# Modulation rows of the first LayerNorm loaded in blocks of 256, 512 and 256 columns, with the first chunk's start re-ordered, in an adaLN transformer block

## The chip, the cores and the metric

One Trainium2 chip, one of its NeuronCores. The metric is the device time in microseconds of one execution. The engines are named as in the profile: PE is TensorE (matrix multiplication), DVE is VectorE, ACT is ScalarE, POOL is GpSimd, SP is SyncE, which in this kernel only issues DMAs.

## What is computed

The reference is one transformer block with adaptive LayerNorm. Its core, cut to what matters:

```python
x = A_x                                             # 1 x 2048 x 1024, bf16
mod = (silu(c) @ w_mod).reshape(1, 6, 1, 1024)      # c: 1 x 1024, w_mod: 1024 x 6144
sa, ca, ga, sb, cb, gb = mod[:, 0] ... mod[:, 5]
h = layernorm(x) * (1 + ca) + sa
q, k, v = split(h @ wqkv)                           # 32 heads of 32
phi = lambda t: where(t > 0, t + 1, exp(t)) + 1e-6
kv = sum over s of phi(k) v;  z = sum over s of phi(k)
o = (phi(q) kv) / (phi(q) z + 1e-6)                 # linear attention
x = x + ga * (o @ wo)
h = layernorm(x) * (1 + cb) + sb
x = x + gb * ((silu(h @ w_gate) * (h @ w_up)) @ w_down)    # hidden width 3584
```

So before the first key can be computed, the kernel needs the LayerNorm statistics of the rows, the two vectors `sa` and `ca` (a matrix-vector product with the first 2048 columns of `w_mod`) and the key part of `wqkv`.

## The kernel before, in words

The 2048 rows of `x` are cut into four chunks of 512 (`NSC`), each of four row tiles of 128 (`STC`); the 1024 features are eight groups of 128 (`DC`), and every matrix product accumulates over these eight in one PSUM bank of 128 x 512. There are eight such banks. The order of all work is written out by hand: the kernel turns automatic scheduling off (line 130), each engine runs its instructions in the order in which the code states them, and only the waits between engines are put in by the framework. From line 423 on, a list `seq` gives the order of the big groups (values, queries, keys of the next chunk, feed-forward) and `put` hangs smaller steps behind them; the change does not touch that part.

What it touches is the head, lines 132 to 420, the first chunk up to its keys.

Loads. SP issues all of them on one queue (lines 133 to 161): `c`, then four row tiles of `x` (256 KB each), then, in turn, a pair of blocks of `w_mod` and two of the eight 128-row pieces of the key weights. `load_wme(p)` loads 256 columns for `ca` and 256 for `sa`, 512 KB each, in runs of 512 bytes; `load_wk(c0, c1)` loads pieces of 256 KB in runs of 2 KB. The first half of the value weights (`load_cols`, runs of 1 KB), row tiles 4 to 7, the other value half and the query weights follow (lines 375 to 381).

Row tiles. For each of the four, DVE takes statistics (`ln_stats`, L196 to L200), POOL makes the inverse deviation and the shift (L202, L204), and the tile is normalised (`ln_xn`): tiles 0, 1 and 3 on ACT (L214), tile 2 on POOL (L211). PE transposes each tile into a PSUM bank (`tr0`, L326; tile st uses bank st), and ACT or DVE copies it to `M4`, which holds the features on the partitions (`tr0_evac`, L332, L334).

Modulation. `mod_mm(p)` (L343) multiplies 256 columns of `ca` and 256 of `sa` with `silu(c)`: 32 matmuls with one moving column each, into a corner of bank 7. `mod_rows(p)` (L349 to L351) copies them out on DVE and adds 1 to `ca`; `modulate` (L224) applies scale and shift to a feature group of `M4` in place.

Keys. `kmm` (L242) is one 128 x 512 matmul of a key group (a row tile and one half of the key columns), for one feature group `cc`. There are eight key groups, 64 such matmuls. Groups 0 to 6 accumulate at once in banks 0 to 6, feature group by feature group, as the weights arrive; between them stand the four `mod_mm` and the transposes of tiles 2 and 3. Group 7 needs bank 7, which the modulation uses, so all its eight matmuls come last (lines 418 to 420). `k_evac` applies phi: ACT exponential (L237), DVE minimum and add (L238), DVE maximum and add (L239). The values (`v_group`, L257) follow at once, eight groups of eight matmuls that go through banks 0 to 4 in turn.

`warm(n)` (L187) issues n matmuls on zeros into bank 7; 21 stand at the start and 3 after the first transpose.

Of the kernel before, what the change touches and what calls it, by code (L numbers as in the profile page):

```python
# [10 lines left out]
BF16 = mybir.dt.bfloat16  # L11
# [10 lines left out]
def kernel(  # L22
# [13 lines left out]
    nc = tc.nc  # L36
    P = nc.NUM_PARTITIONS
    _, S, D = A_x.shape
# [3 lines left out]
    DC = D // P  # L42
# [24 lines left out]
    wm_v = w_mod.rearrange("(p j) n -> p j n", j=DC)  # L67
    c_v = c.rearrange("o (p j) -> p (o j)", j=DC)
# [8 lines left out]
    bank = [psum.tile([P, NB], F32, name=f"bank{i}") for i in range(8)]  # L77
# [9 lines left out]
    def view(region, off, shape, dtype=BF16):  # L87
        n = 1
        for s_ in shape:
            n *= s_  # L90
        w = n * (2 if dtype == F32 else 1)
        ap = region[:, off:off + w]
        if dtype == F32:
            ap = ap.bitcast(F32)
        if len(shape) == 2:
            ap = ap.rearrange("p (a b) -> p a b", a=shape[0])
        elif len(shape) == 3:
            ap = ap.rearrange("p (a b c) -> p a b c", a=shape[0], b=shape[1])
        return ap
# [6 lines left out]
    wme = view(M3, 0, [DC, 2 * D])  # L106
# [24 lines left out]


    c_sb = const.tile([P, DC], BF16, name="c_sb")
    nc.sync.dma_start(out=c_sb[:], in_=c_v)

    def load_x(st):
        nc.sync.dma_start(out=xs[st % 6], in_=x2[st * P:(st + 1) * P, :])

    def load_wme(p):
        for base in (D, 0):  # L140
            s_ = slice(base + p * 256, base + (p + 1) * 256)
            nc.sync.dma_start(out=wme[:, :, s_], in_=wm_v[:, :, s_])  # L142

    def load_wk(c0, c1):
        nc.sync.dma_start(out=wk[:, c0:c1, :], in_=wqkv_v[:, c0:c1, D:2 * D])  # L145

    def load_cols(dst, base, h):
        nc.sync.dma_start(out=dst[:, :, h * NB:(h + 1) * NB],
                          in_=wqkv_v[:, :, base + h * NB:base + (h + 1) * NB])

    for st in range(STC):
        load_x(st)
    load_wme(0)
    load_wk(0, 2)
    load_wme(1)
    load_wk(2, 4)
    load_wme(2)
    load_wk(4, 6)
    load_wme(3)
    load_wk(6, 7)  # L160
    load_wk(7, 8)

# [9 lines left out]
    saT = const.tile([P, DC], BF16, name="saT")  # L172
    ca1T = const.tile([P, DC], BF16, name="ca1T")
    sbT = const.tile([P, DC], BF16, name="sbT")
    cb1T = const.tile([P, DC], BF16, name="cb1T")
    m1 = const.tile([P, 6, DC], BF16, name="m1")
# [5 lines left out]
    scT = const.tile([P, DC], BF16, name="scT")  # L182
# [9 lines left out]
    def ln_stats(st):  # L192
        x_sb = xs[st % 6]
        stats = small.tile([P, NH, nc.vector.BN_STATS_DIM], F32, name="stats")
        for i in range(NH):
            nc.vector.bn_stats(out=stats[:, i, :], in_=x_sb[:, i * NB:(i + 1) * NB])  # L196
        mv = small.tile([P, nc.vector.BN_AGGR_DIM], F32, name="mv")
        nc.vector.bn_aggr(out=mv[:], in_=stats[:])
        veps = small.tile([P, 1], F32, name="veps")
        nc.vector.tensor_scalar_add(out=veps[:], in0=mv[:, 1:2], scalar1=LN_EPS)  # L200
        rstd = small.tile([P, 1], F32, name="rstd")
        nc.gpsimd.tensor_tensor(out=rstd[:], in0=veps[:], in1=neg_half[:], op=ALU.pow)  # L202
        nmr = small.tile([P, 1], F32, name="nmr")
        nc.gpsimd.tensor_scalar(out=nmr[:], in0=mv[:, 0:1], scalar1=rstd[:], scalar2=-1.0,  # L204
                                op0=ALU.mult, op1=ALU.mult)
        stat[st] = (rstd, nmr)

    def ln_xn(st, pool):
        rstd, nmr = stat.pop(st)
        if pool:  # L210
            nc.gpsimd.tensor_scalar(out=xns[st % 6], in0=xs[st % 6], scalar1=rstd[:], scalar2=nmr[:],  # L211
                                    op0=ALU.mult, op1=ALU.add)
        else:
            nc.scalar.activation(out=xns[st % 6], in_=xs[st % 6], func=ACT.Identity, scale=rstd[:], bias=nmr[:])  # L214
# [7 lines left out]
    def modulate(sc_, cc, sT, c1T, c0=0, c1=SCW):  # L222
        h = M4[:, sc_, cc, c0:c1]
        nc.vector.tensor_scalar(out=h, in0=h, scalar1=c1T[:, cc:cc + 1], scalar2=sT[:, cc:cc + 1],  # L224
                                op0=ALU.mult, op1=ALU.add)
# [9 lines left out]
    def phi_to(dst, acc):  # L235
        e = epool.tile([P, NB], F32, name="e")
        nc.scalar.activation(out=e[:], in_=acc, func=ACT.Exp)  # L237
        nc.vector.tensor_scalar(out=e[:], in0=e[:], scalar1=1.0, scalar2=PHI_EPS, op0=ALU.min, op1=ALU.add)  # L238
        nc.vector.scalar_tensor_tensor(out=dst, in0=acc, scalar=0.0, in1=e[:], op0=ALU.max, op1=ALU.add)  # L239

    def kmm(acc, sc_, t, h, cc):
        nc.tensor.matmul(acc[:], lhsT=M4[:, sc_, cc, t * P:(t + 1) * P], rhs=wk[:, cc, h * NB:(h + 1) * NB],  # L242
                         start=(cc == 0), stop=(cc == DC - 1))

    def k_evac(acc, t, h):
        phi_to(pk[:, t, h * NB:(h + 1) * NB], acc[:])
# [74 lines left out]


    def tr0(st):
        tp = bank[st][:].bitcast(BF16).rearrange("p (c s) -> p c s", c=DC)
        for cc in range(DC):
            nc.tensor.transpose(tp[:, cc, :], xns[st][:, cc * P:(cc + 1) * P], ident[:])  # L326

    def tr0_evac(st):
        tp = bank[st][:].bitcast(BF16).rearrange("p (c s) -> p c s", c=DC)
        dst = M4[:, 0, :, st * P:(st + 1) * P]  # L330
        if st % 2 == 0:
            nc.scalar.copy(out=dst, in_=tp)  # L332
        else:
            nc.vector.tensor_copy(out=dst, in_=tp)  # L334

    def mod_mm(p):
        mps = bank[7][:, p * 4:p * 4 + 4]
        for kind, base in enumerate((D, 0)):
            for i in range(2):
                col = base + (2 * p + i) * P  # L340
                o = kind * 2 + i
                for j in range(DC):
                    nc.tensor.matmul(mps[:, o:o + 1], lhsT=wme[:, j, col:col + P], rhs=scT[:, j:j + 1],  # L343
                                     start=(j == 0), stop=(j == DC - 1))

    def mod_rows(p):
        mps = bank[7][:, p * 4:p * 4 + 4]
        c2 = slice(2 * p, 2 * p + 2)
        nc.vector.tensor_copy(out=m1[:, 1, c2], in_=mps[:, 0:2])  # L349
        nc.vector.tensor_copy(out=saT[:, c2], in_=mps[:, 2:4])  # L350
        nc.vector.tensor_scalar_add(out=ca1T[:, c2], in0=m1[:, 1, c2], scalar1=1.0)  # L351

    warm(21)
    for st in range(STC):
        ln_stats(st)
    ln_xn(2, True)
    mask = const.tile([P, KVW], BF16, name="mask")
    nc.gpsimd.memset(mask[:], 0.0)
    for j in range(HPC):
# [3 lines left out]
    nc.gpsimd.memset(v_c[:, :, :, P:VW], 1.0)  # L363
    ln_xn(0, False)
    tr0(0)
    warm(3)
    ln_xn(1, False)
    tr0(1)
    tr0_evac(0)
    tr0_evac(1)  # L370
    mod_mm(0)
    mod_rows(0)
    modulate(0, 0, saT, ca1T, 0, 2 * P)
    modulate(0, 1, saT, ca1T, 0, 2 * P)
    tr0(2)
    ln_xn(3, False)
    load_cols(wv, 2 * D, 0)
    for st in range(STC, STC + 4):
# [1 line left out]
    load_cols(wv, 2 * D, 1)  # L380
    load_cols(wq, 0, 0)
    load_cols(wq, 0, 1)

    tr0_evac(2)
    G = [(t, h) for t in range(STC) for h in range(NH)]
    for g in (0, 1):
        for cc in (0, 1):
            kmm(bank[g], 0, G[g][0], G[g][1], cc)
    tr0(3)
    tr0_evac(3)  # L390
    modulate(0, 0, saT, ca1T, 2 * P, 4 * P)
    modulate(0, 1, saT, ca1T, 2 * P, 4 * P)
    for g in (2, 3):
        for cc in (0, 1):
            kmm(bank[g], 0, G[g][0], G[g][1], cc)
    mod_mm(1)
    mod_rows(1)
    for g in (4, 5, 6):
        for cc in (0, 1):
            kmm(bank[g], 0, G[g][0], G[g][1], cc)  # L400
    modulate(0, 2, saT, ca1T)
    modulate(0, 3, saT, ca1T)
    for p in (1, 2):
        k = 0
        for cc in (2 * p, 2 * p + 1):
            for g in range(7):
                kmm(bank[g], 0, G[g][0], G[g][1], cc)
                k += 1
                if k == 10:
                    mod_mm(p + 1)  # L410
                    mod_rows(p + 1)
                    modulate(0, 2 * p + 2, saT, ca1T)
                    modulate(0, 2 * p + 3, saT, ca1T)
    for g in range(7):
        for cc in (6, 7):
            kmm(bank[g], 0, G[g][0], G[g][1], cc)
        k_evac(bank[g], *G[g])
    for cc in range(DC):
        kmm(bank[7], 0, G[7][0], G[7][1], cc)
    k_evac(bank[7], *G[7])  # L420


    seq = []
# [264 lines left out]
```

## Time and profile before

| | |
|---|---|
| Median of 6 runs (lowest to highest) | 848.66 us (848.07 to 849.27) |
| The profiled execution's own time | 848.69 us |
| Span of its profile | 846.9 us, so 1.8 us lie around the span |
| PE busy | 834.3 us, 99% of the span, 4368 recorded instructions |
| DVE, ACT, POOL busy | 323.1, 143.9, 79.9 us |
| First value matmul (L257) starts | 32.65 us after the start of the span |
| 64 value matmuls | 32.65 to 46.46 us |

The profile's page gives busy time by engine, then the span in 40 slices of 21 us each, with the clock granted to PE and the share of the DMA engines; then the chain of work that ended last, and groups of instructions by source line. The trace behind it answers questions on a stretch of time: the instructions of one engine in order of time, with the idle time ahead of them and what ended it; the busy time of each engine in each of several short windows; and for DMAs the time from issue to landing. A recorded matmul of 128 x 512 lasts 379 ns because matmuls are pipelined; from start to start they take about 216 ns. Some matmuls are missing from the records.

### The profile page before, as it was taken

What the parts mean: (1) busy time and instruction counts of PE and PEld (TensorE: products, weight loads), DVE (VectorE), ACT (ScalarE), POOL (GpSimd) and SP (SyncE); (2) the same over time, 40 slices, a digit from 0 to 9 for tenths busy, and PEclk for the clock granted to TensorE, in tenths of its full rate; (3) what the DMA queues carried; (4) which work ended last, traced back from release to release, by engine and by line L of the source; (5) the groups of instructions that cost most, each with busy time, mean ns of one, the idle gap of its engine ahead of it and who ended that gap; (6) DMA issues with size and microseconds to landing.
All of it is one profiled execution on the core that took longest, in us unless ns stands there. A gap on an engine that the chain in (4) does not pass through costs nothing.

```text
span 846.9 us, 10893 instructions
## 1 busy us (share of the span) xinstructions
PE 834.3 (99%) x4368; PEld 396.6 (47%) x4452; DVE 323.1 (38%) x617; ACT 143.9 (17%) x269; POOL 79.9 (9%) x143
## 2 busy tenths in 40 slices
PE   8999999999999999999999999999999999999998
PEld 4454555544444444444444444444444444444444
DVE  5757455497755655422111221221122122112222
ACT  3333233322311111111111001111000111100000
POOL 2124030014122323100000000000000000000000
PEclk9999999999999999999999999999999999999999
DMA  9984982055489998877875215555322555201220
GB/s 279 317 243 116 283 191 64 1 118 159 98 212 218 217 220 212 193 244 240 246 236 179 69 52 171 149 151 149 106 75 69 151 154 157 86 15 66 75 69 26
DMA packets 203763, 128.65 MB, mean 152 GB/s; under 512 B 50496, under 2 KB 189888, under 8 KB 203712
## 3 DMA queue, kind: packets, MB, share of 16 engines
q1 hardware_dynamic: 163008, 98.58, 40.9%
q10 hardware_dynamic: 38400, 20.98, 11.7%
q0 software_dynamic: 2304, 8.39, 2.6%
q8 instruction: 35, 0.57, 0.3%
q14 instruction: 16, 0.13, 0.1%
HBM read 103.81 MB, written 12.58 MB: 137 GB/s over the span
## 4 chain that ended last, share of the span: by engine, by line
PE 95%; SPq 2%; DVE 1%; DMA 1%; issue 1%; ACT 0%; DVEq 0%
PE bank L515 23%; PE bank L534 23%; PE bank L509 23%; PE bank L466 7%; PE bank L265 6%; PE bank L257 6%; PE bank L242 5%; DMA M<-in_w_mod_dram 1%; SPq L145 1%; PE bank L439 1%; SPq L142 1%; PE bank L274 1%; PE bank L301 1%; DVE stats L196 0%; DVE M L239 0%
## 5 line engine op out<-in xcount | busy, mean ns | idle before, releaser
L515 PE MATMUL bank<-M,M 128*128 128x512 bf16 x881 | 210.4, 379 | 0.8
L509 PE MATMUL bank<-M,M 128*128 128x512 bf16 x871 | 209.7, 379 | 1.3
L517 DVE TENSOR_TENSOR M<-bank,e 128x512 bf16<-128x512 f32 x112 | 77.5, 692 | 275.1 <-PE bank L515 265.7
L534 PE MATMUL bank<-M,M 128*128 128x512 bf16 (+1 forms) x687 | 146.9, 370 | 0.6
L512 ACT ACTIVATE e<-bank 128x512 f32<-128x512 f32 x112 | 66.8, 597 | 439.7 <-PE bank L509 415.7
L534 PEld LDWEIGHTS <-M 128*128 128x128 bf16 x924 | 90.4, 98 | 103.3
L515 PEld LDWEIGHTS <-M 128*128 128x128 bf16 x896 | 87.7, 98 | 105.7
L509 PEld LDWEIGHTS <-M 128*128 128x128 bf16 x896 | 87.3, 98 | 103.9
L538 DVE TENSOR_TENSOR M<-bank,gb_bc 128x512 f32<-128x512 f32 (+1 forms) x33 | 22.3, 676 | 149.2 <-PE bank L534 135.3
L242 PE MATMUL bank<-M,M 128*128 128x512 bf16 x244 | 58.3, 382 | 1.1 <-DVE M L334 0.3
L466 PE MATMUL bank<-M,M 128*128 128x512 bf16 x254 | 57.8, 379 | 0.1
L265 PE MATMUL bank<-M,M 128*128 128x512 bf16 x250 | 56.7, 379 | 0.3
L257 PE MATMUL bank<-M,M 128*128 128x512 bf16 x250 | 56.2, 379 | 0.3
L237 ACT ACTIVATE e<-bank 128x512 f32<-128x512 f32 x64 | 37.8, 598 | 100.2 <-PE bank L265 48.4
L534 PE MATMUL bank<-M 128*128 128x512 bf16 x219 | 50.7, 379 | 0.3
L239 DVE SCALAR_TENSOR_TENSOR M<-bank,e 128x512 bf16<-128x512 f32 x64 | 44.3, 692 | 3.7
L238 DVE TENSOR_SCALAR e<-e 128x512 f32<-128x512 f32 x64 | 27.7, 433 | 41.5 <-ACT e L237 41.3
L466 PEld LDWEIGHTS <-M 128*128 128x128 bf16 x256 | 24.9, 98 | 29.8
L257 PEld LDWEIGHTS <-M 128*128 128x128 bf16 x256 | 24.7, 98 | 29.1
L265 PEld LDWEIGHTS <-M 128*128 128x128 bf16 x256 | 24.6, 98 | 27.9
L242 PEld LDWEIGHTS <-M 128*128 128x128 bf16 x256 | 24.4, 99 | 28.4 <-DVE M L224 1.3
L468 DVE TENSOR_TENSOR M<-bank,M 128x512 f32<-128x512 f32 x32 | 22.1, 690 | 14.5 <-PE bank L466 14.3
(66 smaller groups left out, 335.4 us busy)
## 6 DMA issues: line engine op xcount, KB each, us to landing
M<-in_B_w_gate_dram SPq DMA_DIRECT2D x56, 512.0 KB, 3.9
M<-in_B_w_up_dram SPq DMA_DIRECT2D x56, 512.0 KB, 5.0
M<-in_w_mod_dram SPq DMA_DIRECT2D x8, 1024.0 KB, 6.8
x_scratch<-M POOLq DMA_DIRECT2D x16, 512.0 KB, 6.2
M<-x_scratch ACTq DMA_DIRECT2D x16, 512.0 KB, 3.4
M<-in_B_w_down_dram SPq DMA_DIRECT2D x6, 1024.0 KB, 8.1
M<-in_A_x_dram SPq DMA_DIRECT2D x16, 256.0 KB, 6.8
M<-in_w_mod_dram SPq DMA_DIRECT2D x8, 512.0 KB, 7.7
```

Source lines behind the costliest of these rows:

```text
L237: nc.scalar.activation(out=e[:], in_=acc, func=ACT.Exp)
L238: nc.vector.tensor_scalar(out=e[:], in0=e[:], scalar1=1.0, scalar2=PHI_EPS, op0=ALU.min, op1=ALU.add)
L239: nc.vector.scalar_tensor_tensor(out=dst, in0=acc, scalar=0.0, in1=e[:], op0=ALU.max, op1=ALU.add)
L242: nc.tensor.matmul(acc[:], lhsT=M4[:, sc_, cc, t * P:(t + 1) * P], rhs=wk[:, cc, h * NB:(h + 1) * NB], start=(cc == 0), stop=(cc == DC - 1))
L257: nc.tensor.matmul(acc[:], lhsT=M4[:, sc_, cc, t * P:(t + 1) * P], rhs=wv[:, cc, h * NB:(h + 1) * NB], start=(cc == 0), stop=(cc == DC - 1))
L265: nc.tensor.matmul(acc[:], lhsT=wq[:, cc, qc * P:(qc + 1) * P], rhs=M4[:, sc_, cc, :], start=(cc == 0), stop=(cc == DC - 1))
L466: nc.tensor.matmul(acc[:], lhsT=oTs[st % 3][:, cc, :], rhs=wo[:, cc, hs], start=(cc == 0), stop=(cc == DC - 1))
L509: nc.tensor.matmul(g_ps[:], lhsT=wg_blk[:, cc, fs], rhs=M4[:, sc_, cc, :], start=(cc == 0), stop=(cc == DC - 1))
L512: nc.scalar.activation(out=sg[:], in_=g_ps[:], func=ACT.Silu)
L515: nc.tensor.matmul(u_ps[:], lhsT=wu_blk[:, cc, fs], rhs=M4[:, sc_, cc, :], start=(cc == 0), stop=(cc == DC - 1))
L517: nc.vector.tensor_tensor(out=gus[sc_][:, f, :], in0=u_ps[:], in1=sg[:], op=ALU.mult)
L534: nc.tensor.matmul(y_ps[:, 0:w], lhsT=gus[sc_][:, f, t * P:(t + 1) * P], rhs=wd(f)[:, c0:c1], start=(f == 0), stop=(f == FC - 1))
```

## The change

Four things in the head change.

1. Loads. `c` is issued after the second row tile of `x` instead of first. `load_wme` now takes one of the two kinds and a range of feature groups. `ca` and `sa` are loaded in blocks of 256, 512 and 256 columns each, so that runs are 512, 1024 and 512 bytes; the key weights come in pieces of 2, 3, 1, 1, 1 feature groups instead of 2, 2, 2, 1, 1.
2. Modulation. `mod_mm` and `mod_rows` take one kind and a range of feature groups. The products for `ca` and for `sa` of a block are started each as its own load arrives. The second block gives feature groups 2 to 5 at once.
3. Row tile 2 is normalised on ACT like the others, ahead of tile 3. The transposes use banks 4, 5, 6, 4.
4. Key groups. For feature groups 0 and 1 the loop runs over groups 0 to 3, then 4 to 6. Then both products of the second block, the four modulations, and feature groups 2 to 5 for key groups 0 to 6. Six of the eight matmuls of group 7 are put behind the last `sa` product, ahead of the last two feature groups of all eight groups.

The number of matmuls of every kind stays the same. Line numbers behind line 134 move by two in the changed kernel (L242 becomes L244, L257 becomes L259, L224 becomes L226); `mod_mm` stays at L343, its rows become L349 to L352.

```diff
     for st in range(STC):
         load_x(st)
-    load_wme(0)
+        if st == 1:
+            nc.sync.dma_start(out=c_sb[:], in_=c_v)
+    load_wme(D, 0, 2)
+    load_wme(0, 0, 2)
     load_wk(0, 2)
-    load_wme(1)
-    load_wk(2, 4)
-    load_wme(2)
-    load_wk(4, 6)
-    load_wme(3)
+    load_wme(D, 2, 6)
+    load_wme(0, 2, 6)
+    load_wk(2, 5)
+    load_wme(D, 6, 8)
+    load_wme(0, 6, 8)
+    load_wk(5, 6)
     load_wk(6, 7)
     load_wk(7, 8)
...
-    ln_xn(2, True)
...
     tr0_evac(0)
-    tr0_evac(1)
-    mod_mm(0)
-    mod_rows(0)
-    modulate(0, 0, saT, ca1T, 0, 2 * P)
-    modulate(0, 1, saT, ca1T, 0, 2 * P)
-    tr0(2)
+    ln_xn(2, False)
     ln_xn(3, False)
...
+    tr0_evac(1)
+    mod_mm(0, 0, 2)
+    mod_rows(0, 0, 2)
+    mod_mm(1, 0, 2)
+    mod_rows(1, 0, 2)
+    tr0(2)
     tr0_evac(2)
+    for cc in range(2):
+        modulate(0, cc, saT, ca1T, 0, 2 * P)
     G = [(t, h) for t in range(STC) for h in range(NH)]
-    for g in (0, 1):
-        for cc in (0, 1):
+    for cc in range(2):
+        for g in range(4):
             kmm(bank[g], 0, G[g][0], G[g][1], cc)
...
+        if cc == 0:
+            tr0(3)
+            tr0_evac(3)
+            for c_ in range(2):
+                modulate(0, c_, saT, ca1T, 2 * P, 4 * P)
+    for cc in range(2):
+        for g in range(4, 7):
             kmm(bank[g], 0, G[g][0], G[g][1], cc)
-    mod_mm(1)
-    mod_rows(1)
...
+    mod_mm(0, 2, 6)
+    mod_rows(0, 2, 6)
+    mod_mm(1, 2, 6)
+    mod_rows(1, 2, 6)
+    for cc in range(2, 6):
+        modulate(0, cc, saT, ca1T)
+    for cc in range(2, 6):
+        for g in range(7):
             kmm(bank[g], 0, G[g][0], G[g][1], cc)
...
+        if cc == 4:
+            mod_mm(0, 6, 8)
+            mod_rows(0, 6, 8)
+    mod_mm(1, 6, 8)
+    mod_rows(1, 6, 8)
+    for cc in range(6, 8):
+        modulate(0, cc, saT, ca1T)
+    for cc in range(6):
+        kmm(bank[7], 0, G[7][0], G[7][1], cc)
+    for g in range(8):
+        for cc in range(6, 8):
             kmm(bank[g], 0, G[g][0], G[g][1], cc)
         k_evac(bank[g], *G[g])
-    for cc in range(DC):
-        kmm(bank[7], 0, G[7][0], G[7][1], cc)
-    k_evac(bank[7], *G[7])
```

More of the change, by code (lines that the diff above doesn't have):

```diff
@@ L133, with load_wme @@
     c_sb = const.tile([P, DC], BF16, name="c_sb")
-    nc.sync.dma_start(out=c_sb[:], in_=c_v)
     def load_x(st):
         nc.sync.dma_start(out=xs[st % 6], in_=x2[st * P:(st + 1) * P, :])
[L139 to L142, printed above, removed]
+    def load_wme(base, c0, c1):
+        s_ = slice(base + c0 * P, base + c1 * P)
+        nc.sync.dma_start(out=wme[:, :, s_], in_=wm_v[:, :, s_])
     def load_wk(c0, c1):
@@ L323, in tr0 @@
     def tr0(st):
-        tp = bank[st][:].bitcast(BF16).rearrange("p (c s) -> p c s", c=DC)
+        tp = bank[4 + st % 3][:].bitcast(BF16).rearrange("p (c s) -> p c s", c=DC)
         for cc in range(DC):
@@ L328, in tr0_evac @@
     def tr0_evac(st):
-        tp = bank[st][:].bitcast(BF16).rearrange("p (c s) -> p c s", c=DC)
+        tp = bank[4 + st % 3][:].bitcast(BF16).rearrange("p (c s) -> p c s", c=DC)
         dst = M4[:, 0, :, st * P:(st + 1) * P]
@@ L334, in tr0_evac, with mod_mm, mod_rows @@
             nc.vector.tensor_copy(out=dst, in_=tp)
[L336 to L351, printed above, removed]
+    def mod_mm(kind, c0, c1):
+        for cc in range(c0, c1):
+            o = (2 * cc) + kind
+            col = (0 if kind else D) + cc * P
+            for j in range(DC):
+                nc.tensor.matmul(bank[7][:, o:o + 1], lhsT=wme[:, j, col:col + P], rhs=scT[:, j:j + 1],
+                                 start=(j == 0), stop=(j == DC - 1))
+    def mod_rows(kind, c0, c1):
+        src = bank[7][:, 2 * c0 + kind:2 * c1 + kind:2]
+        if kind:
+            nc.vector.tensor_copy(out=saT[:, c0:c1], in_=src)
+        else:
+            nc.vector.tensor_copy(out=m1[:, 1, c0:c1], in_=src)
+            nc.vector.tensor_scalar_add(out=ca1T[:, c0:c1], in0=m1[:, 1, c0:c1], scalar1=1.0)
     warm(21)
@@ L382 @@
     load_cols(wq, 0, 1)
+    tr0_evac(1)
[4 more added lines that the diff above has]
+    tr0(2)
     tr0_evac(2)
+    for cc in range(2):
+        modulate(0, cc, saT, ca1T, 0, 2 * P)
     G = [(t, h) for t in range(STC) for h in range(NH)]
-    for g in (0, 1):
-        for cc in (0, 1):
+    for cc in range(2):
+        for g in range(4):
             kmm(bank[g], 0, G[g][0], G[g][1], cc)
[L389 to L394, printed above, removed]
-            kmm(bank[g], 0, G[g][0], G[g][1], cc)
-    mod_mm(1)
-    mod_rows(1)
-    for g in (4, 5, 6):
-        for cc in (0, 1):
-            kmm(bank[g], 0, G[g][0], G[g][1], cc)
[L401 to L415, printed above, removed]
+        if cc == 0:
[5 more added lines that the diff above has]
+        for g in range(4, 7):
+            kmm(bank[g], 0, G[g][0], G[g][1], cc)
+    mod_mm(0, 2, 6)
[6 more added lines that the diff above has]
+        for g in range(7):
+            kmm(bank[g], 0, G[g][0], G[g][1], cc)
+        if cc == 4:
[9 more added lines that the diff above has]
+        for cc in range(6, 8):
             kmm(bank[g], 0, G[g][0], G[g][1], cc)
         k_evac(bank[g], *G[g])
-    for cc in range(DC):
-        kmm(bank[7], 0, G[7][0], G[7][1], cc)
-    k_evac(bank[7], *G[7])
     seq = []
```

## The prediction, made before the result

> **What bounds the kernel now.** I read the page's busy times first, then PE's waits, then PE's instructions in order of time over the head, the windows with the granted clock, and the DMAs' times to landing.
>
> The page says that PE is the bound of the whole:
>
> ```profile
> span 846.9 us, 10893 instructions
> PE 834.3 (99%) x4368; PEld 396.6 (47%) x4452; DVE 323.1 (38%) x617; ACT 143.9 (17%) x269; POOL 79.9 (9%) x143
> ```
>
> The change removes no matmul, so it can only move the time at which PE, from then on without a gap, starts the value groups. In the trace this is the first L257 matmul, at 32.65 us. PE in order of time up to there (start, length, idle time ahead in brackets):
>
> ```profile
> 9.43 0.62 PE L326 MATMUL bank<-ident,M 128*128 128x128 bf16 x8 [0.18 <-ACT M L214]
> 9.89 0.54 PE L343 MATMUL bank<-scT,M 128*128 128x1 bf16 x16
> 11.44 0.55 PE L343 MATMUL bank<-scT,M 128*128 128x1 bf16 x16 [1.01 <-DMA M<-in_w_mod_dram]
> 12.57 1.01 PE L326 MATMUL bank<-ident,M 128*128 128x128 bf16 x8 [0.58 <-POOL M L211]
> ...
> 17.35 0.94 PE L343 MATMUL bank<-scT,M 128*128 128x1 bf16 x32
> 18.15 3.61 PE L242 MATMUL bank<-M,M 128*128 128x512 bf16 x15
> 21.60 0.94 PE L343 MATMUL bank<-scT,M 128*128 128x1 bf16 x32
> 22.41 3.38 PE L242 MATMUL bank<-M,M 128*128 128x512 bf16 x13
> 25.62 0.54 PE L343 MATMUL bank<-scT,M 128*128 128x1 bf16 x16
> 26.32 0.55 PE L343 MATMUL bank<-scT,M 128*128 128x1 bf16 x16 [0.16 <-DMA M<-in_w_mod_dram]
> 26.73 6.08 PE L242 MATMUL bank<-M,M 128*128 128x512 bf16 x25
> 32.65 3.62 PE L257 MATMUL bank<-M,M 128*128 128x512 bf16 x16
> ```
>
> PE's waits here are short, but the chain that ended last shows one long piece, "DMA M<-in_w_mod_dram" from 18.29 to 26.27 us, ahead of the last `sa` product. So the head is paced by loads: the last `sa` block lands at 26.29, and behind it stand 16 products and 26 key matmuls. Until there PE has only just enough to do. The windows show what the earlier gaps did (stretch; PE, PEld, DVE, ACT, POOL busy; granted clock; DMA share, GB/s):
>
> ```profile
> 10.00:12.00 2.00, 0.98 (x33) 0.81 (x30) 0.91 (x3) 0.90 (x2) 1.47 (x3) 1.00 1.12 331
> 12.00:14.00 2.00, 1.43 (x9) 1.11 (x11) 1.26 (x5) 1.01 (x2) 1.47 (x11) 0.66 1.20 291
> 14.00:16.00 2.00, 1.78 (x12) 1.23 (x11) 0.00 (x0) 1.91 (x2) 0.00 (x0) 0.50 1.07 339
> 16.00:18.00 2.00, 1.67 (x32) 1.02 (x30) 1.29 (x3) 0.00 (x0) 0.00 (x0) 0.99 1.16 312
> ```
>
> From 12.67 to about 16.08 the clock was 0.50. The queue is full throughout (share over 1, about 300 to 340 GB/s), so loads land in order of issue and bytes decide.
>
> **Landing times.** Issue plus time to landing gives, before: last `x` tile 6.4, first `ca` 9.66, first `sa` 11.36, keys 0-1 12.76, then `ca` 14.58, `sa` 16.35, keys 2-3 17.76, `ca` 19.53, `sa` 21.33, keys 4-5 22.74, `ca` 24.5, `sa` 26.29. A 512 KB block in 512-byte runs therefore takes 1.77 us, 512 KB of keys in 2 KB runs 1.41. For 1 KB runs of the same matrix the trace has the three late blocks of `w_mod`, 1 MB each, issued at 50.34, about 50.9 and 51.7:
>
> ```profile
> M<-in_w_mod_dram SPq DMA_DIRECT2D x1, 1024.0 KB, 6.2
> ```
> ```profile
> M<-in_w_mod_dram SPq DMA_DIRECT2D x1, 1024.0 KB, 8.5
> ```
> ```profile
> M<-in_w_mod_dram SPq DMA_DIRECT2D x1, 1024.0 KB, 10.8
> ```
>
> They land at 56.5, 59.4 and 62.5: 3.0 us per MB, against 3.54 for two 512-byte blocks.
>
> **Loads of the changed kernel.** `x` tile 0 is issued at about 0.73 instead of 1.17, as `c` (0.39 us of SP) no longer precedes it; `c` itself is 2 KB. That brings everything forward by 0 to 0.44; I take 0.3. First `sa` 11.06; keys 0-1 +1.41 = 12.47; `ca` 2-5 +3.0 = 15.5; `sa` 2-5 +3.0 = 18.5; keys 2-4 (768 KB in 2 KB runs) +2.1 = 20.6; then `ca` 6-7 22.4, `sa` 6-7 24.1, keys 5, 6, 7 at 24.8, 25.5, 26.2. All of the set is in 1.4 us earlier than the 27.6 of before. But a DMA counts as landed only whole, and feature group 2 of the keys now stands behind 3 instead of 2 MB of modulation, and in one DMA with groups 3 and 4.
>
> Here the Trainium skill speaks against the change: "DMA: Bandwidth & Descriptors", Specifications, puts the least transfer for line rate at 512 bytes, so by it the longer runs bring nothing and the two big blocks take 3.54 each: keys 2-4 would land at 21.7. The trace has 1.77 against about 1.5 us for the same bytes of this matrix, so I take the row; the rule's 1.1 us more goes into the range.
>
> **PE of the changed kernel.** Products for `sa` run at 11.1 to 11.6. Tile 2: DVE's statistics start 0.44 earlier, ACT does tile 1 until 9.0, the copy of tile 0 (0.99) until 9.9, tile 2 (1.24) until 11.2, tile 3 until 12.4, where before POOL had tile 2 ready at 12.51 because it stood behind the shift of tile 3. The 0.58 us wait goes and nothing new waits: behind tile 2 on ACT stand only tile 3 and a copy, both ahead of need. POOL loses one 1.19 us operation that nobody else awaits. `c` lands by about 5, ahead of ACT's first tile at 6.2; were it later, it would hold ACT's queue. But all this is worth nothing by itself, since the keys 0-1 land at 12.47 and the wait only moves there. The 14 key matmuls of groups 0 and 1 (0.216 each, 3.0 us), tile 3's transpose (0.6) and its copy end at about 16.4 at full clock (18 at half). Then 32 `ca` products (0.80 by 17.35 to 18.15) until 17.2, a wait of 1.2 us for `sa` at 18.5, 32 products until 19.3; copy and first modulation (before: 22.54 to 23.35, about 0.7) until 20.0; and a wait until the keys land at 20.6. Before, PE had done about 19 key matmuls and 64 products by 20.6 (11 from 18.15 on, at 0.216); now it has done 14 and 96.
>
> **The sum.** Behind 20.6: 50 key matmuls x 0.2158 (value groups: 64 in 13.81) = 10.8; 32 products 0.8; the matmul into bank 7 waits for DVE's `sa` copy out of that bank, 0.25; start 0.1. Total 11.9, so the values start at 32.5, against 32.65. The six matmuls of group 7 (1.3 us) cover the last two modulations (about 1.0); before, four matmuls covered them and some 0.3 us of waiting remained at 27.8 to 28.1, so this part gains nothing net of the 0.25. By loads alone: 0.1 us gained.
>
> **The clock** decides the rest. PE waits twice between 17.2 and 20.6, 1.2 + 1.3 us, and 0.8 us of the rest is one-column products. By the skill ("TensorE: Matmul & The Clock Gate", the HAM clock gate) the clock falls after a whole idle window of about 3.4 us; no gap is as long, so 0 lost. The trace has 0.50 for 3.4 us after gaps of only 1.01 and 0.58 (1.65 of the preceding 3.4 us busy), so I take the row. The windows run on their own phase, so the half clock covers between 0.9 and 3.4 us behind the wait, and half of that is lost: 0.45 to 1.7, middle 1.1. Should the early half clock of before come back, the 14 matmuls run until 18, the waits shrink and nothing more is lost. Expected: -0.1 + 1.1 = 1.0 us on 848.69, so 849.6 (this execution is within 0.03 of the median).
>
> **Behind the head.** Evacuations of the eight groups start when group 0 is done, 3.0 us ahead of the values (14 matmuls), before 4.1. The first chain, 0.60 + 0.43 + 0.69, frees bank 0 1.2 us ahead of the first value group, and each next one takes 1.06 against 1.73 per value group: hidden; with that cover gone it would cost the remainder of 1.7. DVE's statistics of tiles 4 to 7 move from 37.6 by about 1 us; the next keys start at 62.2 and their modulations end at 59.0, so this is hidden too. SP's later loads land 1 us or more earlier than before; their first user is at 32.5.
>
> **Rivals.** No clock lost (30%): the half clock comes early or not at all; 848.3 to 848.9, not slower. For it: the changed early part is busier, so the balance may hold. Against it: two gaps within 3.4 us. Slower (25%): the large key DMA lands late, at 21 to 21.7 (no head start, 512-byte and 1 KB runs alike), and a whole 3.4 us at half clock follows: +0.4 to 1.2 and +1.7, so 850.4 to 851.5; it decides once the landing plus half the cold time exceeds 22.4. Faster by over 0.2% would need the keys at 19.0, so 3.4 MB in 7.9 us, 430 GB/s; the best window shows 381, which gives 19.9 and 847.9. I leave 5% for what I don't see. The likeliest (40%) is 849.1 to 850.3, some clock lost behind the wait.
>
> **How the numbers follow.** 0.2% is 1.7 us, about what a measurement of this kernel can tell from no change. Faster 0.05 is the last case; slower 0.25 the third; the rest, 0.70, is the first two. The range, 847.9 to 851.1, takes in the best load rate and most of the slow case.
>
> **What would show it.** Right: PE waits for a `w_mod` DMA near 17 to 18.5 and for the key DMA until about 20.6; PE clock 0.5 in a window behind it; first value matmul at 33 to 34; no wait for POOL at a transpose; the rest unchanged. Wrong: value start before 31 (loads faster than any row here), a wait at the first value group for DVE (evacuation not hidden), or a second stretch at half clock behind 24.

## The result and the profile after

The changed kernel takes 851.12 us in the median of 16 runs (848.35 to 853.01), the kernel before 848.68 in the median of 37 (848.07 to 849.27). The ratio is 1.0025 with a 95% interval of 1.0019 to 1.0032: slower by a quarter of a per cent, and spread over 4.7 us where the kernel before spreads over 1.2. The profiled execution took 851.44 us, its span 849.6. The forecast of 849.6 had the direction and less than half of the loss; the median stands at the very edge of the stated range, 851.1.

The page still has PE as the bound, with its busy time 1.0 us longer and 2.7 us more span:

```profile
span 849.6 us, 10888 instructions
PE 835.3 (98%) x4369; PEld 396.5 (47%) x4452; DVE 322.8 (38%) x614; ACT 144.8 (17%) x270; POOL 78.8 (9%) x142
```

PE in order of time over the head (start, length, idle time ahead and what ended it):

```profile
9.54 0.54 PE L343 MATMUL bank<-scT,M 128*128 128x1 bf16 x16
10.65 0.54 PE L343 MATMUL bank<-scT,M 128*128 128x1 bf16 x16 [0.57 <-DVE m L351]
11.06 0.62 PE L328 MATMUL bank<-ident,M 128*128 128x128 bf16 x8
11.91 1.04 PE L244 MATMUL bank<-M,M 128*128 128x512 bf16 x3 [0.23 <-DVE M L226]
...
15.94 0.94 PE L343 MATMUL bank<-scT,M 128*128 128x1 bf16 x32
17.55 0.95 PE L343 MATMUL bank<-scT,M 128*128 128x1 bf16 x32 [0.67 <-DMA M<-in_w_mod_dram]
20.43 0.59 PE L244 MATMUL bank<-M,M 128*128 128x512 bf16 x1 [1.93 <-DMA M<-in_A_wqkv_dram]
21.24 6.77 PE L244 MATMUL bank<-M,M 128*128 128x512 bf16 x19 [0.22 <-issue]
27.85 0.54 PE L343 MATMUL bank<-scT,M 128*128 128x1 bf16 x16
28.25 1.67 PE L244 MATMUL bank<-M,M 128*128 128x512 bf16 x7
29.76 0.54 PE L343 MATMUL bank<-scT,M 128*128 128x1 bf16 x16
30.55 4.91 PE L244 MATMUL bank<-M,M 128*128 128x512 bf16 x21 [0.25 <-DVE saT L349]
35.30 4.91 PE L259 MATMUL bank<-M,M 128*128 128x512 bf16 x22
```

Read it against the same view of before. The wait for POOL at a transpose is gone. Two waits for loads have come, 0.67 us at the second `sa` block and 1.93 us at key pieces 2 to 4. Behind the second, the first 21 key matmuls take from 20.43 to 27.85, 7.4 us, where 21 x 0.216 would be 4.5. The first value matmul starts at 35.30 instead of 32.65: 2.65 us, all of the span's 2.7. The prediction had named 33 to 34.

The windows, cut where the clock changes (stretch; PE, PEld, DVE, ACT, POOL busy; granted clock; DMA share, GB/s), say why:

```profile
9.24:12.66 3.42, 2.57 (x52) 2.02 (x51) 2.23 (x9) 3.42 (x4) 1.93 (x13) 1.00 1.04 364
12.66:16.07 3.41, 3.03 (x26) 1.48 (x25) 1.29 (x3) 1.73 (x2) 0.00 (x0) 1.00 1.10 350
16.07:19.48 3.41, 1.76 (x65) 1.68 (x62) 1.24 (x6) 0.00 (x0) 0.00 (x0) 1.00 1.09 356
19.48:22.90 3.42, 2.25 (x5) 0.84 (x6) 0.64 (x2) 0.00 (x0) 0.00 (x0) 0.50 1.16 312
22.90:26.31 3.41, 3.41 (x9) 1.18 (x8) 0.00 (x0) 0.00 (x0) 0.00 (x0) 0.50 1.03 353
26.31:29.72 3.41, 3.41 (x31) 1.77 (x30) 0.33 (x2) 0.00 (x0) 0.00 (x0) 1.00 1.07 375
```

The stretch with the waits has 1.76 us of PE work in 3.41, and the next two stretches run at 0.50. The first of these, 2.25 us busy, starts with the rest of the wait and does not bring the clock back; the second, full, does. From 20.43 to 26.31 that is 5.88 us of work at half clock, and half of it, 2.94 us, is lost. The profiled execution is no exception in this: 9 of the 16 runs have a mean clock of 0.995 or 0.996 as it has (0.996), which is about two stretches of half clock in 850 us, and they took 850.34 to 853.01. The mean clock does not order the runs by itself: those at 0.998, about one stretch, took from 848.49 to 851.43, so where the stretch lies and how late the loads land count too.

The loads: keys 2 to 4, issued at 8.70, took

```profile
M<-in_A_wqkv_dram SPq DMA_DIRECT2D x1, 768.0 KB, 11.7
```

to landing, so they landed at 20.4.

### The profile page after: what moved, and what is told of

It reads as the page before. It is cut to its first block, busy times and chain, and to the rows that moved or that the text cites. A ratio compares the mean times of both kernels' runs of the same rounds, so it can differ in the third digit from the quotient of the medians.

```text
span 849.6 us, 10888 instructions
## 1 busy us (share of the span) xinstructions
PE 835.3 (98%) x4369; PEld 396.5 (47%) x4452; DVE 322.8 (38%) x614; ACT 144.8 (17%) x270; POOL 78.8 (9%) x142
## 4 chain that ended last, share of the span: by engine, by line
PE 95%; DVE 1%; DMA 1%; SPq 1%; issue 1%; ACT 0%; DVEq 0%
PE bank L515 23%; PE bank L534 23%; PE bank L509 23%; PE bank L466 6%; PE bank L267 6%; PE bank L259 6%; PE bank L244 6%; DMA M<-in_A_wqkv_dram 1%; PE bank L439 1%; PE bank L276 1%; PE bank L303 1%; SPq L140 0%; DVE stats L198 0%; DVE M L241 0%; DVE e L240 0%
## 5 line engine op out<-in xcount | busy, mean ns | idle before, releaser
L244 PE MATMUL bank<-M,M 128*128 128x512 bf16 x245 | 60.0, 392 | 3.5 <-DMA M<-in_A_wqkv_dram 1.9
L259 PE MATMUL bank<-M,M 128*128 128x512 bf16 x250 | 56.2, 379 | 0.3
L244 PEld LDWEIGHTS <-M 128*128 128x128 bf16 x256 | 24.9, 100 | 32.4 <-issue 5.3
L259 PEld LDWEIGHTS <-M 128*128 128x128 bf16 x256 | 24.7, 98 | 29.1
L267 PEld LDWEIGHTS <-M 128*128 128x128 bf16 x256 | 24.6, 98 | 27.9
L468 DVE TENSOR_TENSOR M<-bank,M 128x512 f32<-128x512 f32 x32 | 22.1, 690 | 14.5 <-PE bank L466 14.3
```

The costliest lines, as they stand in the source:

```text
L267: nc.tensor.matmul(acc[:], lhsT=wq[:, cc, qc * P:(qc + 1) * P], rhs=M4[:, sc_, cc, :], start=(cc == 0), stop=(cc == DC - 1))
```

## Experiments

**Theory:** behind the head nothing changes; the values start 11.9 us after PE begins feature group 2, and later by half of the time that PE spends at half clock behind that point. The loads set that point, and the waits for them bring the half clock, in some executions and not in others. **Rivals:** the late whole-block loads alone are the loss; or it is PE's new order (tile 2, bank 7, evacuations). While testing, a third came up: that the small load of `c` stalls the queue. Each experiment is timed against the kernel before on the same chip; ratios are with their 95% intervals. "Zero matmuls" are 384 columns of zeros into unused columns of bank 7.

### The waits covered with zero matmuls

```diff
     mod_rows(0, 2, 6)
+    fill(3)
     mod_mm(1, 2, 6)
     mod_rows(1, 2, 6)
+    fill(11)
```

> The changed kernel with 3 matmuls on zeros (384 columns, into unused columns of bank 7) behind the ca product of the second block and 11 behind its sa product, so that PE is busy through the two waits for loads; no load and no other instruction moves. Clock theory (the waits of 0.7 and 1.9 us bring 0.50 clock for up to 6.8 us, and 0.5 us is lost per us of it): no half clock behind 17 us, first value matmul at 32.3 to 32.6, 848.3 to 848.6 us, and a spread of about 1 us instead of 4.7. Load rival (the late key DMA itself is what costs): nothing changes, 851.1. Evacuation or bank-7 rival: 851.1 too.

Measured: 851.59 us in the median of 6 (848.81 to 851.8), ratio 1.0032 (1.0020 to 1.0043). By the median the theory failed. But the one profiled execution was the 848.81, and it did what the theory asked:

```profile
17.27 0.65 PE L356 MATMUL bank<-zt 128*128 128x384 bf16 x3 [0.25 <-DVE m L351]
17.75 0.94 PE L343 MATMUL bank<-scT,M 128*128 128x1 bf16 x32
18.94 1.95 PE L356 MATMUL bank<-zt 128*128 128x384 bf16 x11 [0.25 <-DVE saT L349]
20.75 4.69 PE L244 MATMUL bank<-M,M 128*128 128x512 bf16 x21
...
32.73 5.56 PE L259 MATMUL bank<-M,M 128*128 128x512 bf16 x25
```

The clock is 1.00 throughout from 8 us on, the 21 key matmuls take 4.5 us (20.75 to 25.28), and keys 2 to 4 landed at 20.7 (issued at 9.18, 11.5 us to landing), no earlier than the 20.4 of the changed kernel. So in this execution loads as late as those, with the clock held, did not make 851. What the other five executions did, this trace does not show; a later experiment shows one way.

### Key pieces 2, 3 and 4 as three loads, alone and with zero matmuls

```diff
-    load_wk(2, 5)
+    load_wk(2, 3)
+    load_wk(3, 4)
+    load_wk(4, 5)
```

> The changed kernel with the key pieces 2, 3 and 4 as three DMAs of 256 KB instead of one of 768 KB, same order and bytes. If the whole-DMA wait matters: piece 2 lands about 1.4 us ahead of 20.4, PE's second wait falls from 1.9 to about 0.5 us, the values start at 31.3 to 31.6 when the clock stays full, so about 847.5, and the half clock is rarer; median 847.5 to 849. If only the total of bytes matters, or the clock falls on the first wait alone: 850.5 to 851.1.

Measured: 849.93 in the median of 21 (848.51 to 851.3), ratio 1.0014 (1.0007 to 1.0020). In its trace:

```profile
18.31 0.95 PE L345 MATMUL bank<-scT,M 128*128 128x1 bf16 x32 [0.93 <-DMA M<-in_w_mod_dram]
19.97 6.39 PE L246 MATMUL bank<-M,M 128*128 128x512 bf16 x21 [0.71 <-DVE M L228]
...
33.65 4.70 PE L261 MATMUL bank<-M,M 128*128 128x512 bf16 x21
```

The key wait is gone; PE waits 0.71 us for DVE's modulation instead. The one DMA for three pieces was part of the loss: the median is 1.2 us below that of the change. It is still above the expected 847.5 to 849; in the trace 3.4 us at half clock follow (20.46 to 23.87).

With 3 zero matmuls in each wait as well:

> Both: key pieces 2 to 4 as three DMAs, and 3 zero matmuls in each of the two waits. Clock theory: the split's 1 us is kept in every run, 847.3 to 847.8 with a spread of about 1 us, and faster than the kernel before by 0.8 to 1.4 us. Load rival: the same as the split alone.

Measured: 849.21 in the median of 22 (847.61 to 852.43), ratio 1.0010 (1.0003 to 1.0016), so neither the time nor the narrow spread that was expected. The five executions with a mean clock of 1.0 took 847.6 to 848.6, the rest 848.6 to 852.4. The profiled one, at 851.0, is of the rest: its loads came late from the start (first keys at 13.3, in the changed kernel 11.6), and half clock held from 21.2 to 24.6.

### The half clock of the kernel before taken away

```diff
+            if p == 0 and kind == 1:
+                fill(5)
...
     modulate(0, 1, saT, ca1T, 0, 2 * P)
+    fill(3)
     tr0(2)
```

> The kernel before with 5 zero matmuls between its first ca and sa products and 3 ahead of the transpose of row tile 2, the two gaps ahead of its 0.50 clock at 12.7 to 16.1. If that half clock is hidden because the loads pace the head (the last sa block at 26.3): no change, 848.4 to 848.8. If it costs what half clock costs, 1.7 us: about 847.0.

Measured: 848.52 (848.23 to 850.2, 13 runs), ratio 1.0001 (0.9993 to 1.0009). In its trace the clock is 1.00 where before it was 0.50, and PE then waits 0.80 us for the last `sa` block instead of 0.16:

```profile
26.14 0.55 PE L345 MATMUL bank<-scT,M 128*128 128x1 bf16 x16 [0.80 <-DMA M<-in_w_mod_dram]
...
32.47 5.77 PE L257 MATMUL bank<-M,M 128*128 128x512 bf16 x26
```

The values begin 0.2 us earlier than before (32.65), and the time is the same. A stretch of half clock ahead of the last load cost nothing here; behind the loads it cost half of its length.

### The place of c

```diff
     c_sb = const.tile([P, DC], BF16, name="c_sb")
+    nc.sync.dma_start(out=c_sb[:], in_=c_v)
...
-        if st == 1:
-            nc.sync.dma_start(out=c_sb[:], in_=c_v)
```

> The changed kernel with c loaded first again, ahead of the row tiles of x, all else as changed. Stall theory (the 2 KB load of c, 16 bytes per partition, in the middle of the big loads holds the queue for 0 to 1.7 us, differently in each execution; the trace of the filled and split kernel has only 202 to 269 GB/s from 5 to 8 us and the first key pieces at 13.3 instead of 11.6): the slowest runs vanish, median about 850, what is left is the half clock behind the two waits. Clock-only theory: c's place costs nothing, 851 to 851.5 (0.44 us later loads), spread as before.

Measured: 850.23 (848.52 to 852.2, 21 runs), ratio 1.0017 (1.0011 to 1.0024). The interval overlaps that of the change, and the slowest runs have not vanished; the median lies between the two expectations. Its profiled execution, 849.17, happens to show the third way that the change can go, with the half clock early (12.5 to 15.9):

```profile
12.47 1.89 PE L243 MATMUL bank<-M,M 128*128 128x512 bf16 x4 [0.23 <-DVE M L225]
...
19.17 0.95 PE L342 MATMUL bank<-scT,M 128*128 128x1 bf16 x32 [0.47 <-DMA M<-in_w_mod_dram]
21.12 4.69 PE L243 MATMUL bank<-M,M 128*128 128x512 bf16 x21 [1.00 <-DVE M L225]
...
33.10 5.13 PE L258 MATMUL bank<-M,M 128*128 128x512 bf16 x23
```

The first four key matmuls take twice as long, the first wait shrinks to 0.47 us, the second is one for DVE, and no half clock follows.

The converse, `c` behind the second row tile in the kernel before, the same diff the other way round:

> The kernel before with this one part of the change alone: c loaded behind the second row tile of x. Stall theory: loads land 0 to 1.7 us later, less the 0.44 us of head start, and the last sa block paces the head, so the median rises to 849.0 to 849.8 and the spread from 1.5 to 2 or 3 us. Clock-only theory: 848.2 to 848.6, by up to 0.44 us faster, same spread.

Measured: 848.48 (847.94 to 849.89, 13 runs), ratio 1.0001 (0.9993 to 1.0009). No loss from this part alone, where the stall theory asked for 849.0 or more.

### c first with zero matmuls

The two diffs above on the kernel with 3 and 11 zero matmuls, and on the split one with 3 and 3.

> The changed kernel with c first and the 3 and 11 zero matmuls in the two waits. If stall and half clock are the two causes: both gone, 848.4 to 849.0 with a spread of about 1 us. Clock-only: as the filled kernel, 851.6. If something else holds it: above 850.

Measured: 850.25 (849.15 to 851.95, 8 runs), ratio 1.0021 (1.0010 to 1.0031), in two heaps: four runs at 849.15 to 849.5 with a mean clock of 0.999 to 1.0, four at 851.0 to 851.95 with 0.996 to 0.998. Even the lower heap does not lie within the expected 848.4 to 849.0. The profiled run is of the upper heap, and shows one way in which the cover of the first experiment can fail:

```profile
17.68 0.65 PE L355 MATMUL bank<-zt 128*128 128x384 bf16 x3 [0.25 <-DVE m L350]
19.20 0.95 PE L342 MATMUL bank<-scT,M 128*128 128x1 bf16 x32 [0.87 <-DMA M<-in_w_mod_dram]
20.40 3.58 PE L355 MATMUL bank<-zt 128*128 128x384 bf16 x11 [0.25 <-DVE saT L348]
23.82 4.70 PE L243 MATMUL bank<-M,M 128*128 128x512 bf16 x21
...
35.80 2.54 PE L258 MATMUL bank<-M,M 128*128 128x512 bf16 x11
```

The `sa` block landed 1.6 us later than in the trace of the change, three zero matmuls were too few, 0.87 us stayed idle, the clock fell at 20.3, and now the 11 zero matmuls themselves took 3.58 us instead of 1.95 and held the real work until 23.82. A cover that is too short in one place is paid for twice.

> c first, key pieces 2 to 4 as three DMAs, 3 zero matmuls in each wait. If stall and half clock are the two causes: 847.5 to 848.2, narrow, and faster than the kernel before by about 0.5 to 1 us. Clock-only: 849.2, as without c first.

Measured: 849.12 (847.82 to 851.02, 13 runs), ratio 1.0004 (0.9995 to 1.0012): five runs at 847.8 to 848.3 with clock 1.0, eight at 849.0 to 851.0 below it. The median is that of the same kernel without `c` first (849.21), as the clock alone asks.

### A longer cover

```diff
     mod_rows(0, 0, 2)
+    fill(3)
     mod_mm(1, 0, 2)
...
     mod_rows(0, 2, 6)
+    fill(10)
     mod_mm(1, 2, 6)
     mod_rows(1, 2, 6)
+    fill(10)
```

> The changed kernel, loads untouched, with 3, 10 and 10 zero matmuls in the same three places. They cover 3.2 us of the two waits, 0.6 more than these waits last, so the values start up to 0.9 us later than 32.3 when the loads land early. Clock theory: 848.6 to 849.4 with a spread of about 1 us, against 851.1 with 4.7; the runs at 851 to 852 of the kernel with 3 and 11 were those in which the loads came later and the cover was too short. Load theory (late loads alone make 851): 851 to 852 stay in half the runs.

Measured: 850.39, ratio 1.0020 (1.0012 to 1.0027), and a spread of 0.59 us (850.16 to 850.75, 17 runs); the mean clock is 0.999 or 1.0 in every one. With the waits covered and the clock held, the changed kernel with its own loads is as steady as the kernel before. The median is 1.0 us above the expectation, and the trace shows that it is the cover's own length:

```profile
17.67 1.78 PE L356 MATMUL bank<-zt 128*128 128x384 bf16 x10 [0.25 <-DVE m L351]
19.29 0.94 PE L343 MATMUL bank<-scT,M 128*128 128x1 bf16 x32
20.49 1.78 PE L356 MATMUL bank<-zt 128*128 128x384 bf16 x10 [0.25 <-DVE saT L349]
22.11 4.70 PE L244 MATMUL bank<-M,M 128*128 128x512 bf16 x21
...
34.09 4.26 PE L259 MATMUL bank<-M,M 128*128 128x512 bf16 x19
```

Feature group 2 begins at 22.11, when the zero matmuls end, and the values follow 11.98 us later.

The split loads with 3, 8 and 4 in the same places:

> The changed kernel with key pieces 2 to 4 as three DMAs and more zero matmuls: 3 between the first ca and sa products, 8 in the wait for the second sa block, 4 behind it, so that the wait is covered even when the loads land 1 us later than in the trace of the change. Clock theory: half clock in few runs, 847.8 to 848.6, spread about 1 us; at or below the kernel before. If the number of idle microseconds ahead of the wait is not what decides the clock: 849.2 as with 3 and 3.

Measured: 849.05 (848.54 to 851.77, 13 runs), ratio 1.0005 (0.9997 to 1.0013). Twelve of 13 runs lie within 1.1 us, with clock 0.999 or 1.0; the one at 851.77 has 0.998. Steadier than with 3 and 3, but no faster than the kernel before and above the expected 847.8 to 848.6, for the same reason: group 2 begins at 20.65, when the cover ends.

### Parts of the change on the kernel before

Row tile 2 on ACT, and six matmuls of group 7 ahead of the last two feature groups:

```diff
-    ln_xn(2, True)
...
     tr0_evac(0)
+    ln_xn(2, False)
...
-    for g in range(7):
+    for cc in range(6):
+        kmm(bank[7], 0, G[7][0], G[7][1], cc)
+    for g in range(8):
         for cc in (6, 7):
...
-    for cc in range(DC):
-        kmm(bank[7], 0, G[7][0], G[7][1], cc)
-    k_evac(bank[7], *G[7])
```

> The kernel before with two parts of the change alone: row tile 2 on ACT, and six of group 7's matmuls ahead of the last two feature groups. By my sum: the 0.35 us wait of 27.8 to 28.1 for the modulation goes, a wait of up to 0.25 for bank 7 may come, the tile's 0.58 us wait moves to a load: 848.3 to 848.6, spread as before. If one of these parts carries the loss: above 849.5.

Measured: 848.52 (847.89 to 849.05, 13 runs), ratio 0.9998 (0.9990 to 1.0006). These two parts carry no loss. The rest of PE's new order was not run without the new loads. The trace has a small gain that the median cannot prove, 5.61 us from the first key matmul behind the last products to the values, where before it was 5.92 (26.73 to 32.65):

```profile
26.20 0.55 PE L343 MATMUL bank<-scT,M 128*128 128x1 bf16 x16 [0.59 <-DMA M<-in_w_mod_dram]
26.62 5.77 PE L242 MATMUL bank<-M,M 128*128 128x512 bf16 x26
32.23 5.99 PE L257 MATMUL bank<-M,M 128*128 128x512 bf16 x27
```

The loads alone:

```diff
-    load_wme(0)
-    load_wk(0, 2)
-    load_wme(1)
-    load_wk(2, 4)
...
+    load_wme(D, 0, 2)
+    load_wme(0, 0, 2)
+    load_wk(0, 2)
+    load_wme(D, 2, 6)
+    load_wme(0, 2, 6)
+    load_wk(2, 5)
...
```

> The kernel before with the changed blocks and key pieces alone (256, 512, 256; 2, 3, 1, 1, 1), PE's order and c as before. If the whole-block loads are the cause: PE waits for the second sa block until 18 to 19 and for keys 2 to 4 until about 20.8 with only half its work done, then half clock follows: 849.5 to 851.5 and a spread of several us. If PE's new order is the cause: 848.6.

Measured: 849.95 (849.56 to 852.8, 14 runs), ratio 1.0018 (1.0010 to 1.0025), and no run with a mean clock above 0.998.

```profile
15.94 0.54 PE L344 MATMUL bank<-scT,M 128*128 128x1 bf16 x16
17.95 0.57 PE L344 MATMUL bank<-scT,M 128*128 128x1 bf16 x16 [1.48 <-DMA M<-in_w_mod_dram]
18.39 5.23 PE L243 MATMUL bank<-M,M 128*128 128x512 bf16 x16
...
34.19 4.05 PE L258 MATMUL bank<-M,M 128*128 128x512 bf16 x18
```

PE waits 1.48 us for the 512-column `sa` block, and the half clock runs from 18.0 to 21.4, over the 16 matmuls behind it: 5.2 us for what takes 3.6 before. The values begin 1.54 us later than before (34.19 against 32.65), close to half of that stretch. So the new loads alone make a loss, in the old order of PE too: 1.2 us by the medians, where the whole change loses 2.4.

### One table over all traces

From the executions profiled; us from the start of the span. Half clock is what lies behind the start of feature group 2. The sum is that start, plus 11.9, plus half of that.

| kernel | group 2 begins | half clock behind it | sum | values begin | span |
|---|---|---|---|---|---|
| the change | 20.43 | 5.88 | 35.3 | 35.30 | 849.6 |
| 3 and 11 zero matmuls | 20.75 | 0 | 32.7 | 32.73 | 847.0 |
| split keys | 19.97 | 3.4 | 33.6 | 33.65 | 847.8 |
| split, 3 and 3 | 21.54 | 3.1 | 35.0 | 35.05 | 849.2 |
| c first | 21.12 | 0 | 33.0 | 33.10 | 847.4 |
| c first, 3 and 11 | 23.82 | 0 | 35.7 | 35.80 | 850.1 |
| c first, split, 3 and 3 | 21.42 | 3.4 | 35.0 | 35.09 | 849.2 |
| split, 3, 8 and 4 | 20.65 | 0 | 32.6 | 32.63 | 846.8 |
| 3, 10 and 10 | 22.11 | 0 | 34.0 | 34.09 | 848.4 |

In all nine the sum is within 0.1 us, and span less start of the values is 814.1 to 814.3, as it is for the kernel before (814.25) and its four variants. All of each difference lies ahead of the values.

## Why the forecast was right and where it was too small

**Loads.** Keys 2 to 4 were put at 20.6 and landed at 20.4, but partly by luck. The first `sa` products ran at 10.65 instead of 11.1 and the first keys landed at 11.6 instead of 12.5; the `sa` block followed at 17.5 instead of 18.5; the three key pieces then took 2.9 us instead of 2.1. The two big blocks took 3.0 us each (11.6 to 17.5), as the row of the late blocks had said; the 3.54 that follow from the Trainium skill's rule ("DMA: Bandwidth & Descriptors", Specifications: full rate from 512 bytes on) did not come. In other traces the first keys landed between 11.6 and 13.3; the forecast allowed 0 to 0.44 for this.

**Work behind the landing.** Forecast 11.9 us; measured 11.98 in each of the five traces without half clock behind the start of group 2. The wait of 0.25 for bank 7 is in every trace as costed, and the cover of the last modulations gained the 0.3 of waiting (5.92 to 5.61 in the trace with two parts of the change).

**Tile 2, POOL, evacuation, statistics behind the head.** Nothing, as forecast: the wait for POOL went, tile 2 on ACT and the moved group 7 on the kernel before give 0.9998, and 814.1 to 814.3 us follow the start of the values in every trace.

**The clock.** Here the forecast took the trace of the kernel before against the rule of a whole idle window (the Trainium skill, "TensorE: Matmul & The Clock Gate", the HAM clock gate), and the trace was right: gaps of 0.67 and 1.93 us, none near 3.4, brought half clock. The size failed. The step said that half clock "covers between 0.9 and 3.4 us behind the wait"; the trace has 5.88, because a stretch that begins with the rest of the wait (2.25 of 3.42 us busy) did not bring the clock back, so two stretches of 3.41 us were lost and not one. The term is 2.9 us instead of 1.1; 849.6 with 1.8 more is 851.4, the time of the profiled execution. The prediction's own list counted "a second stretch at half clock behind 24" as a sign of being wrong, and it came, from 22.90 to 26.31. So the mechanism was right, and this term was put at less than half of what was measured. That the median still met the range is partly luck: 8 of the 16 runs lie above 851.1.

**Rivals.** All three ways appear among the runs, in other shares than forecast. The likeliest band, 849.1 to 850.3, holds one run of 16. No clock lost was put at 848.3 to 848.9: the one run with a mean clock of 1.0 took 848.35. Slower was put at 850.4 to 851.5, with 25%: it should have been the likeliest, since 11 of the 16 runs are above 850.4, seven in its band and four above 851.5, where nothing was named. Its mechanism named late loads and a whole 3.4 us; the trace of the change has the doubled stretch instead, and the trace of the split kernel with 3 and 3 has late loads and one stretch. The early half clock, said to cost nothing more, is the trace with `c` first.

**What loses the clock.** PE's busy share does not tell. Of the stretches of 3.41 us ahead of a half clock, PE was busy for a share of 0.46 to 0.71, but stretches of 0.53, 0.57 and 0.65 were followed by full clock. Two stretches of the split kernel with 3 and 3; full clock follows the first, half clock the second:

```profile
10.97:14.38 3.41, 1.94 (x32) 1.38 (x31) 0.76 (x3) 3.35 (x3) 0.81 (x10) 1.00 1.03 351
17.80:21.21 3.41, 2.41 (x58) 1.71 (x55) 0.82 (x4) 0.00 (x0) 0.00 (x0) 1.00 1.11 329
```

The same two for the one-column products (L345) alone:

```profile
10.97:14.38 3.41, 0.44 (x16) 0.34 (x14) 1.00 1.03 351
17.80:21.21 3.41, 1.46 (x53) 1.28 (x49) 1.00 1.11 329
```

Without these products PE was busy for 1.50 us in the first and 0.95 in the second. That order holds in all nine traces with a half clock. Counted so, the nine stretches ahead of it have 0.00 us (the change), 0.49, 0.56 (the kernel before), 0.65, 0.80, 0.95, 0.98, 1.15 and 1.17; every stretch at full clock between 5 and 45 us that was followed by full clock has 1.48 or more. At half clock, the stretch with 2.25 us (the change, 19.48 to 22.90) was followed by another, those with 2.79 or more by full clock. So in these traces the one-column products fill PE's busy time but do not hold its clock. This is a sorting of traces after the fact; no run varied the products by themselves.

**What stays open.** Where the stretches fall in an execution, which none of the runs controls. Open too is why the first keys land up to 1.7 us apart; the place of `c` was tried and is not shown to be the cause.

## What to carry to other kernels

Where a head is paced by loads, look at what each load releases: merging blocks brought all of the data in earlier and the first usable piece later, and a piece that many matmuls wait for should be a load of its own. A wait of one or two microseconds is priced by the clock behind it, up to twice over and differently in each execution, so compare many runs and place half clock in the trace: in these traces it was free ahead of the last wait for a load, and half of it was lost behind. When asking whether PE is busy enough to keep its clock, leave one-column matmuls out of the count. Filling a wait with idle matmuls held the clock in every run only where it covered the latest landing, and then its length was what one paid.

## What the runs showed of the hardware

Half clock came in stretches of 3.41 us that begin at any phase (12.5, 12.6, 13.2, 18.0, 19.5, 20.3, 20.5, 21.2 and 22.1 us in nine traces), and once two in a row. From full clock it came only behind stretches with at most 1.17 us of PE work other than one-column matmuls, and behind none with 1.48 or more. The same queue of loads, in the same order, delivered its first key pieces between 11.6 and 13.3 us. Blocks of `w_mod` in 1 KB runs moved at 3.0 us per MB, in 512-byte runs at 3.5 (the kernel before).
